# Batch 0 and the end of chunk 0 of a fused attention and GELU-MLP kernel: TensorE's order written anew

## The chip, the cores and the metric

The kernel runs on one core of one Trainium2 chip. The metric is the device time of one execution in microseconds (us). The six runs of the kernel before lie between 326.59 and 328.40 us, with a median of 327.44 us.

## The reference

```python
# q, k, v: (8, 8, 576, 64), s: (8, 8, 576): batch, head, position, width
scores = q @ k^T / 8
cum    = cumsum(max(s, 0))                       # along the positions
scores = where(causal, -1e9, scores + min(cum[j] - cum[i], 0))
attn   = softmax(scores)
x      = (attn @ v) as (4608 tokens, 512)        # token = batch * 576 + position
out    = gelu(x @ w_in) @ w_out                  # w_in: 512 x 2048, w_out: 2048 x 512
```

Eight batches of attention, with a decaying bias, feed a two-layer MLP over 4608 tokens.

## The kernel before, in words

**Attention.** The heads of a batch are taken in four pairs (0 to 3). For a pair, `sc_item` computes the scores, transposed, in two units (u0 and u1), each in a PSUM tile of two banks, tag "sc", of which there are two. ScalarE takes the exponential of each unit (line 415) into a bf16 tile P, and VectorE zeroes what is not causal with a mask (lines 424 and 429). The bias is carried in two weights, `wb` (the exponential of the running sum) and `vv` (v times that). `av_mm` (line 437) then makes either the denominators (P times wb, "den") or the numerators (P times vv, "num"): eight matmuls each for the first 512 positions. `norm_act` takes the denominators on ScalarE through a Ln (two instructions, line 453) and an Exp (line 457), and `norm_dve` (line 480, VectorE, two or three instructions) multiplies numerators by these and writes a pair's rows of `xT`, the input of the MLP. The last 64 positions of a batch are done apart (`av_rest`, `norm_rest`).

With `av_banks(True)`, a pair's numerators and denominators share one "sc" tile (the profile calls it avw). Else they are two one-bank tiles of tag "av" (avn and avd), of which there are three; with `last=True` the numerators take the one bank of tag "mlp". A numerator matmul into an avw tile waits until the Ln has read the denominators out of that tile.

**MLP.** The tokens are cut into nine chunks of 512. `l1_item(c, f2)` (line 541) makes two of the 16 blocks of the hidden layer: 16 matmuls over four rows of `w_in` (row ko needs pair ko of `xT`, and there are two blocks and two column halves e), in an "sc" tile, or with `av=True` in two "av" tiles; a GELU (lines 548, 551) writes them to `gT`. `k0` and `k1` choose rows, so that an item can be made in parts. `l2_item(c, sub, f0, f1)` (line 563) makes 128 rows of the output in a bank, over blocks f0 to f1 of `gT`; `l2_out` copies the bank to SBUF on VectorE (line 573; three buffers o_sb) and stores it through SP's queue (line 575).

**Order.** Nothing is planned by a scheduler: the order in which the program writes instructions is the order of each engine, and each engine runs its own list in order, with semaphore waits where data or a buffer is needed. Attention of batch c+1 is written between the second layer's items of chunk c, so that TensorE has work while ScalarE and VectorE are at the softmax.

- Batch 0 (lines 644 to 653): pairs 0 and 1 use avw tiles, pair 2 avd and avn, pair 3 avd and the "mlp" bank. First the denominators of all, then the numerators of pairs 0, 1, 2, 3, each followed by its `norm_dve`.
- Chunk 0's first layer (lines 657 to 662): two tiles are open, with rows 0 and 1 first, then row 2, then row 3; then the third tile, in the "av" banks.
- Chunk 0's second layer (lines 679 to 743) holds batch 1's attention. Pairs 2 and 3 of batch 1 come at the end (lines 714 to 732).

**The feed of q and k.** From batch 2 on, q and k are loaded (line 105, POOL's queue), interleaved (line 181; batch 2 on POOL, later ones on VectorE), written to DRAM (line 190, SP's queue) and read back transposed into `qkT` (line 197, SP's queue). A tiny POOL copy, `pace`, holds back the next loads: at line 719 until batch 1's last P is masked, at line 740 until the last transposed rows of batch 2 have landed; `load_qk(3)` and `load_v(3)` stand behind that one (lines 741, 742). Batch 3's q is interleaved on VectorE at line 781 in chunk 1, ahead of the masks of the last pair of batch 2.

Of the kernel before, what the change touches and what calls it, by code (L numbers as in the profile page):

```python
# [19 lines left out]
def kernel(  # L20
# [412 lines left out]
    def av_mm(b, p, out, parts, den):  # L433
        for n_part, (jt, lo, n, off) in enumerate(parts):
            for e in range(2):
                h = 2 * p + e
                nc.tensor.matmul(  # L437
                    out[e * 64 : e * 64 + 64, lo : lo + n],
                    lhsT=(
                        wb[:, jt, b * H + h : b * H + h + 1].to_broadcast([128, 64])  # L440
                        if den else vv[b % 2][:, jt, h, :]
                    ),
                    rhs=P_of[b, p][:, e, off : off + n],
                    start=(n_part == 0), stop=n_part == len(parts) - 1,
                    skip_group_check=True,
                )
# [12 lines left out]
    def norm_act(den, w, chunks):  # L459
        ln = norm_ln(den, chunks)  # L460
        norm_exp(ln, w)
        return ln
# [90 lines left out]
    def l2_item(c, sub, f0=0, f1=FT, av=False, defer=False):  # L553

        gT = gT_of[c]
        if f0 == 0:
            tag, bufs = ("av", 3) if av else ("mlp", 1)
            o_of[c, sub] = ps.tile([128, KO * 128], fp32, tag=tag, bufs=bufs, name="o_ps")
        o_ps = o_of[c, sub]
        for ft in range(f0, f1):  # L560
            for e in range(2):
                t0 = sub * 128 + e * 64
                nc.tensor.matmul(  # L563
                    o_ps[e * 64 : e * 64 + 64], lhsT=gT[:, ft, t0 : t0 + 64], rhs=w_out_r[:, ft, :],
                    start=(ft == 0), stop=(ft == FT - 1), skip_group_check=True,
                )
        if f1 == FT and not defer:
            l2_out(c, sub)
# [12 lines left out]
    def gelu_set():  # L581
        nc.scalar.preload_act_table_set("gelu_and_others")
# [63 lines left out]
        av_mm(0, p, avs[p][1], MAIN, True)  # L646
    lns = {p: norm_act(avs[p][1], CUT, CHUNKS) for p in (0, 1)}
    for p in range(NP):
        av_mm(0, p, avs[p][0], MAIN, False)
        norm_dve(0, p, p + 1, avs[p][0], lns[p], 0, CUT, CHUNKS)  # L650
        if p + 2 < NP:
            lns[p + 2] = norm_act(avs[p + 2][1], CUT, CHUNKS)
    gelu_set()

    for c in range(NCH):
        nb = c + 1
        for k0, k1 in ((0, 2), (2, 3)) if c == 0 else ((0, 3),):
            l1_item(c, 0, k0, k1)
            l1_item(c, 1, k0, k1)
        l1_item(c, 0, KO - 1)  # L660
        l1_item(c, 1, KO - 1)
        l1_item(c, 2, av=True)
        if 0 < c and nb < B:
            scale_v(nb, STS, nc.vector)
            absmax_v(nb)
        if c == 0:
            absmax_v(0)
            scale_v(0, STS[ST - 1 :], nc.vector)
        if c < B:
            for p in range(NP):  # L670
                absmax(c, p)
        if 1 < c and nb + 1 < B:
            nc.gpsimd.tensor_copy(pace, qkT[nb % 2][:, 1, NP - 1, 0:1])  # L673
            load_v(nb + 1)
            if nb + 2 < B:
                load_qk(nb + 2)
        for f2 in range(3, FT // 2):
            l1_item(c, f2)
        if c == 0:
            load_v(2)  # L680
            for p in range(NP):
                av_rest(0, p)
            tr_full(1, 0, (nc.vector.tensor_copy, nc.vector.tensor_copy))
            tr_full(1, 1, (nc.scalar.copy, nc.vector.tensor_copy))
            exp_set()
            l2_item(c, 0, 0, 4)
            l2_item(c, 1, 0, 4, av=True)
            norm_rest(0)
            l2_item(c, 0, 4, 8)
            sc_item(1, 0)  # L690
            l2_item(c, 1, 4, 8)
            l2_item(c, 0, 8, 12)
            sc_item(1, 1)
            l2_item(c, 1, 8, 12)
            l2_item(c, 2, 0, 12, av=True)
            scale_pair(1, 0)
            scale_pair(1, 1)
            avs = [av_banks(True) for _ in range(2)]
            for p in (0, 1):
                av_mm(1, p, avs[p][1], MAIN, True)  # L700
            lns = [norm_ln(avs[p][1], CHUNKS) for p in (0, 1)]
            for p in (0, 1):
                norm_exp(lns[p], CUT)
            l2_item(c, 3, 0, 4, av=True)
            for p in (0, 1):
                av_mm(1, p, avs[p][0], MAIN, False)
                norm_dve(1, p, p + 1, avs[p][0], lns[p], 0, CUT, CHUNKS)
            l2_item(c, 3, 4, 8)
            for p in (2, 3):
                tr_full(1, p, (nc.scalar.copy, nc.vector.tensor_copy))  # L710
            scale_pair(1, 2)
            scale_pair(1, 3)
            l2_item(c, 3, 8, 12)
            sc_item(1, 2)
            l2_item(c, 0, 12, defer=True)
            sc_item(1, 3, units=(0,))
            l2_item(c, 1, 12, defer=True)
            sc_item(1, 3, units=(1,))
            nc.gpsimd.tensor_copy(pace, P_of[1, 3][:, 0, UO[1] + 448 : UO[1] + 449])
            interleave(2, "q")  # L720
            interleave(2, "k")
            avs = {}
            for p in (2, 3):
                avs[p] = av_banks(True)
                av_mm(1, p, avs[p][1], MAIN, True)
                ln = norm_act(avs[p][1], CUT, CHUNKS)
                av_mm(1, p, avs[p][0], MAIN, False)
                l2_item(c, p, 12, defer=True)
                l2_out(c, p - 2)
                norm_dve(1, p, p + 1, avs[p][0], ln, 0, CUT, CHUNKS)  # L730
            l2_out(c, 2)
            l2_out(c, 3)
            for i in (0, 1):
                write_rows(2, i, nc.sync)
            for p in (0, 1):
                transpose_rows(2, p)
            gelu_set()
            for p in (2, 3):
                transpose_rows(2, p)
            nc.gpsimd.tensor_copy(pace, qkT[0][:, 1, 3, 0:1])  # L740
            load_qk(3)
            load_v(3)
            absmax_v(1)
        elif nb < B:
            exp_set()
            l2_item(c, 0, 0, 4)
            if c == 1:
                for p in range(NP):
                    av_rest(1, p)
            sc_item(nb, 0)  # L750
            if c == 1:
                norm_rest(1)
            l2_item(c, 0, 4)
            late = c < 3
            for p in range(1, NP):
                if nb + 1 < B and p == 1 and not late:
                    interleave(nb + 1, "q")
                    write_rows(nb + 1, 0, nc.sync)
                if nb + 1 < B and p > 1 and not late:
                    transpose_rows(nb + 1, p - 2)  # L760
                sc_item(nb, p)
                av_item(nb, p - 1)
                if nb + 1 < B and p == NP - 1 and late:
                    interleave(nb + 1, "k")
                    write_rows(nb + 1, 1, nc.sync)
                l2_item(c, p, 0, 12)
                if p == NP - 1:
                    if nb + 1 < B:
                        for pt in range(0 if late else p - 1, NP):
                            transpose_rows(nb + 1, pt)  # L770
                    if c == 1:
                        nc.gpsimd.tensor_copy(pace, qkT[(nb + 1) % 2][:, 1, p, 0:1])
                        load_qk(nb + 2)
                    av_item(nb, p)
                    norm_rest(nb)
                    gelu_set()
                l2_item(c, p, 12)
                if nb == B - 1 and p == 1:
                    cert_decay()
                if nb + 1 < B and p == 2 and late:  # L780
                    interleave(nb + 1, "q")
                    write_rows(nb + 1, 0, nc.sync)
                if nb + 1 < B and p == 1 and not late:
                    interleave(nb + 1, "k")
                    write_rows(nb + 1, 1, nc.sync)
        else:
            if c == B - 1:
                cert_1()
            for sub in range(4):
                if c == NCH - 1 and sub == 2:  # L790
                    break
                l2_item(c, sub, av=sub % 2 == 0)
                if c == B - 1 and sub < 3:
                    (cert_2, cert_3, cert_4)[sub]()
# [174 lines left out]
```

## Time and profile before

| what | value |
|---|---|
| median of 6 runs | 327.44 us (326.59 to 328.40) |
| the profiled execution | 328.12 us, its span 326.1 us |
| granted TensorE clock, mean | 0.999 |
| PE busy | 315.5 us, 97% of the span |
| ACT busy | 204.0 us, 63% |
| DVE busy | 191.9 us, 59% |
| DMA over the span, HBM | 164 GB/s |

PE is TensorE's matmuls, PEld its weight loads, DVE VectorE, ACT ScalarE, POOL GpSimd; SPq and POOLq are the sequencers that issue DMAs. A line of the timeline holds the start in us from the span's start, the duration in us, the engine, the program's line and operation, the tiles (out<-in), the count, and in brackets how long the engine had been idle before it and what ended that. In the view of waits a line holds who waited for whom, the total in us, how many times, and the longest. In the chain of work that ended last, each piece is followed back to what released it.

A matmul's end is modelled, so that one group overlaps the next on the page. In the timeline at single instructions, the starts show more: a group of eight numerators or denominators takes 0.38 us from its first start to the next group's, and 128 first-layer matmuls take 13.81 us in the chain, 0.108 each.

### The profile page before, as it was taken

The page shows a single profiled execution, that of the slowest core. Times are in us where ns is not written, and L with a number is a line of the kernel's source. Part 1 is how long each engine was busy: PE and PEld are TensorE (multiplying, and loading weights), DVE is VectorE, ACT ScalarE, POOL GpSimd, SP SyncE. Part 2 cuts the span into 40 slices and gives each one's busy share as a digit, 9 for nine tenths or more (in the row PEclk, how much of TensorE's full clock was granted, in tenths as well). Part 3 has the DMA queues.
Part 4 walks back from the last instruction along what each step waited for, and adds up shares of the span by engine and source line. Part 5 has one row for each costly group of instructions (what it writes and reads, how often), then busy time and mean ns, then how long its engine had stood idle before and what let it go on. Part 6 is the DMA issues. An engine that isn't in the chain of part 4 may idle for free.

```text
span 326.1 us, 8609 instructions
## 1 busy us (share of the span) xinstructions
PE 315.5 (97%) x3681; PEld 184.4 (57%) x3681; DVE 191.9 (59%) x380; ACT 204.0 (63%) x290; POOL 70.9 (22%) x107
## 2 busy tenths in 40 slices
PE   7999998999999999999999999999999999999994
PEld 3666664666655556556655665556555655455553
DVE  6876558895589247936494749555874672150011
ACT  4896757659576857677667767676759676105400
POOL 8745364304400361008005300410000000000000
PEclk9999999999999999999999999999999999999999
DMA  7999999764985599977995997677600100010012
GB/s 116 213 208 212 232 197 230 276 112 49 255 268 94 110 220 261 216 134 195 252 198 150 206 242 112 121 211 175 111 32 34 66 35 2 32 66 33 3 66 72
DMA packets 53869, 47.45 MB, mean 146 GB/s; under 512 B 31360, under 2 KB 43904, under 8 KB 53824
## 3 DMA queue, kind: packets, MB, share of 16 engines
q0 software_dynamic: 15968, 23.07, 38.4%
q1 hardware_dynamic: 37856, 23.75, 29.8%
q8 instruction: 31, 0.51, 0.7%
q14 instruction: 14, 0.11, 0.1%
HBM read 36.85 MB, written 16.52 MB: 164 GB/s over the span
## 4 chain that ended last, share of the span: by engine, by line
PE 92%; ACT 3%; DMA 2%; POOL 1%; DVE 1%; issue 0%; POOLq 0%
PE h_ps L541 38%; PE o_ps L563 36%; PE sc_ps L399 5%; PE avd L437 3%; PE avn L437 3%; PE lo_ps L809 2%; DMA early_k<-in_q_dram 2%; PE avw L437 1%; PE avr L437 1%; ACT P L415 1%; POOL early_q L117 1%; ACT ln L453 1%; PE tr_ps L363 1%; DVE qkT L384 0%; PE trf_ps L380 0%
## 5 line engine op out<-in xcount | busy, mean ns | idle before, releaser
L563 PE MATMUL o_ps<-w_out_r,gT 128*64 128x512 bf16 x1088 | 126.5, 380 | 0.0
L541 PE MATMUL h_ps<-xT,w_in_r 128*64 128x512 bf16 x1152 | 126.0, 379 | 0.0
L541 PEld LDWEIGHTS <-w_in_r 128*64 128x64 bf16 x1152 | 68.6, 110 | 55.6 <-issue 0.2
L548 ACT ACTIVATE gT<-h_ps 128x1024 bf16<-128x1024 f32 x54 | 54.3, 1023 | 53.8 <-PE h_ps L541 53.8
L563 PEld LDWEIGHTS <-gT 128*64 128x64 bf16 x1088 | 59.4, 110 | 47.5 <-issue 0.2
L415 ACT ACTIVATE P<-sc_ps 128x1024 bf16<-128x1024 f32 x64 | 62.3, 1021 | 26.6 <-PE sc_ps L399 26.1
L424 DVE TENSOR_TENSOR P<-P,tri_bf 128x512 bf16<-128x512 bf16 x59 | 24.6, 423 | 43.7 <-ACT P L415 43.4
L573 DVE COPY o_sb<-o_ps 128x512 f32<-128x512 f32 x34 | 23.4, 687 | 44.4 <-PE o_ps L563 44.2
L216 DVE TENSOR_REDUCE amx<-qkT 128x2 f32<-128x1152 bf16 x32 | 40.9, 1335 | 0.0
L205 POOL DMA_DIRECT2D raw_v<-in_v_dram x40 | 34.3, 882 | 6.9 <-DMA w_in_r<-in_moe_w_in_dram 3.4
L480 DVE SCALAR_TENSOR_TENSOR xT<-avn,ln 128x256 bf16<-128x256 f32 (+3 forms) x60 | 20.2, 383 | 20.1 <-ACT ln L457 14.3
L233 DVE TENSOR_TENSOR vv<-raw_v,wb 128x512 bf16<-128x512 f32 (+3 forms) x44 | 25.3, 633 | 0.1
L223 DVE TENSOR_REDUCE amv<-raw_v 128x1 f32<-128x2048 f32 (+1 forms) x16 | 23.0, 1471 | 3.4 <-DMA raw_v<-in_v_dram 3.4
L457 ACT ACTIVATE ln<-ln 128x512 f32<-128x512 f32 (+1 forms) x40 | 23.4, 588 | 1.2
L551 ACT ACTIVATE gT<-h_ps 128x512 bf16<-128x512 f32 x36 | 19.6, 602 | 6.3 <-PE h_ps L541 6.3
L399 PE MATMUL sc_ps<-qkT 64*128 64x256 bf16 (+2 forms) x320 | 21.3, 250 | 0.7 <-DVE qkT L384 0.3
L399 PEld LDWEIGHTS <-qkT 64*128 64x128 bf16 x320 | 13.0, 94 | 15.2 <-issue 12.8
L453 ACT ACTIVATE ln<-avd 128x256 f32<-128x256 f32 x52 | 17.2, 391 | 6.3 <-PE avd L437 6.3
L437 PEld LDWEIGHTS <-vv 128*64 128x64 bf16 x384 | 17.8, 110 | 3.7 <-issue 2.7
L437 PEld LDWEIGHTS <-wb 128*64 128x64 bf16 x384 | 17.1, 110 | 4.0 <-issue 0.3
L673 POOL CAST pace<-qkT 128x1 f32<-128x1 bf16 x4 | 0.8, 199 | 69.6 <-DMA qkT<-rows 69.6
L437 PE MATMUL avd<-P,wb 128*64 128x256 bf16 x208 | 14.8, 264 | 0.0
(106 smaller groups left out, 184.2 us busy)
## 6 DMA issues: line engine op xcount, KB each, us to landing
out_dram<-o_sb SPq DMA_DIRECT2D x34, 256.0 KB, 2.6
raw_v<-in_v_dram POOLq DMA_DIRECT2D x32, 256.0 KB, 8.4
rows<-qk_bf SPq DMA_DIRECT2D x12, 576.0 KB, 6.7
early_q<-in_q_dram POOLq DMA_DIRECT2D x13, 288.0 KB, 9.5
early_k<-in_k_dram POOLq DMA_DIRECT2D x12, 288.0 KB, 10.0
w_in_r<-in_moe_w_in_dram POOLq DMA_DIRECT2D x4, 512.0 KB, 11.5
w_out_r<-in_moe_w_out_dram POOLq DMA_DIRECT2D x4, 512.0 KB, 12.8
raw_v<-in_v_dram POOLq DMA_DIRECT2D x8, 128.0 KB, 9.4
```

The costliest lines, as they stand in the source:

```text
L205: nc.gpsimd.dma_start(out=t[:n_st, st, :, :], in_=bass.AP(tensor=v.tensor, offset=v.offset + b * H * S * D + st * 128 * D, ap=[[D, n_st], ...
L216: nc.vector.tensor_reduce(amx[:, b * NP + p], qkT[b % 2][:, :, p, :S], axis=AX, op=ALU.max, apply_absolute_value=True)
L233: eng.tensor_tensor(vb[:n_st, st0:st1, h0:h1, :], t[:n_st, st0:st1, h0:h1, :], wb[:n_st, st0:st1, b * H + h0 : b * H + h1] .unsqueeze(3).t ...
L399: nc.tensor.matmul(s_ps[:, e, off : off + n], lhsT=qkT[b % 2][e * 64 : e * 64 + 64, 1, p, jt * 128 : jt * 128 + 128], rhs=qkT[b % 2][e * 6 ...
L415: nc.scalar.activation(P[:, :, UO[u] : UO[u] + UW[u]], s_ps[:, :, : UW[u]], func=AF.Exp, scale=scale)
L424: eng.tensor_tensor(d, d, tri_bf.unsqueeze(1).unsqueeze(1).to_broadcast([128, 2, 2, 128]), op=MULT)
L437: nc.tensor.matmul(out[e * 64 : e * 64 + 64, lo : lo + n], lhsT=(wb[:, jt, b * H + h : b * H + h + 1].to_broadcast([128, 64]) if den else ...
L457: nc.scalar.activation(ln[:, :w], ln[:, :w], func=AF.Exp, scale=-1.0)
L541: nc.tensor.matmul(h_of[c, f2][i][e * 64 : e * 64 + 64], lhsT=w_in_r[:, ko, ft * 128 + e * 64 : ft * 128 + e * 64 + 64], rhs=xT[:, ko, c * ...
L548: nc.scalar.activation(gT_of[c][:, f2 * 2 : f2 * 2 + 2, :], hh_of[c, f2], func=AF.Gelu)
L563: nc.tensor.matmul(o_ps[e * 64 : e * 64 + 64], lhsT=gT[:, ft, t0 : t0 + 64], rhs=w_out_r[:, ft, :], start=(ft == 0), stop=(ft == FT - 1), ...
L573: nc.vector.tensor_copy(o_sb, o_ps)
```

## The change

Three places of the written order change; no instruction is added or removed, and the instructions on VectorE, ScalarE, GpSimd and SP keep their order. Only TensorE's list is in another order.

1. Batch 0: the numerators of pair 2 come ahead of those of pair 1.
2. Chunk 0's first layer: rows 0, 1 and 2 one by one over the two open tiles, and the third tile is opened, with its row 0, ahead of row 3.
3. End of chunk 0: the last four blocks of output sub-block 1 are cut in two, with the scores of pair 3's second unit between them. Both avw tiles of pairs 2 and 3 are taken ahead of the loop; the last quarter of output 2 goes between the two groups of denominators, and that of output 3 between the two groups of numerators.

```diff
     for p in range(NP):
-        av_mm(0, p, avs[p][0], MAIN, False)
+        if p != 2:
+            av_mm(0, p, avs[p][0], MAIN, False)
         norm_dve(0, p, p + 1, avs[p][0], lns[p], 0, CUT, CHUNKS)
         if p + 2 < NP:
             lns[p + 2] = norm_act(avs[p + 2][1], CUT, CHUNKS)
+        if p == 0:
+            av_mm(0, 2, avs[2][0], MAIN, False)
     gelu_set()
...
-        for k0, k1 in ((0, 2), (2, 3)) if c == 0 else ((0, 3),):
+        for k0, k1 in ((0, 1), (1, 2), (2, 3)) if c == 0 else ((0, 3),):
             l1_item(c, 0, k0, k1)
             l1_item(c, 1, k0, k1)
+        if c == 0:
+            l1_item(c, 2, 0, 1, av=True)
         l1_item(c, 0, KO - 1)
         l1_item(c, 1, KO - 1)
-        l1_item(c, 2, av=True)
+        l1_item(c, 2, 1 if c == 0 else 0, av=True)
...
             sc_item(1, 3, units=(0,))
-            l2_item(c, 1, 12, defer=True)
+            l2_item(c, 1, 12, 14)
             sc_item(1, 3, units=(1,))
+            l2_item(c, 1, 14, defer=True)
             nc.gpsimd.tensor_copy(pace, P_of[1, 3][:, 0, UO[1] + 448 : UO[1] + 449])
             interleave(2, "q")
             interleave(2, "k")
-            avs = {}
+            avs = {p: av_banks(True) for p in (2, 3)}
+            lns = {}
             for p in (2, 3):
-                avs[p] = av_banks(True)
                 av_mm(1, p, avs[p][1], MAIN, True)
-                ln = norm_act(avs[p][1], CUT, CHUNKS)
-                av_mm(1, p, avs[p][0], MAIN, False)
-                l2_item(c, p, 12, defer=True)
-                l2_out(c, p - 2)
-                norm_dve(1, p, p + 1, avs[p][0], ln, 0, CUT, CHUNKS)
+                lns[p] = norm_act(avs[p][1], CUT, CHUNKS)
+                if p == 2:
+                    l2_item(c, 2, 12, defer=True)
+            l2_out(c, 0)
+            av_mm(1, 2, avs[2][0], MAIN, False)
+            l2_item(c, 3, 12, defer=True)
+            norm_dve(1, 2, 3, avs[2][0], lns[2], 0, CUT, CHUNKS)
+            l2_out(c, 1)
+            av_mm(1, 3, avs[3][0], MAIN, False)
+            norm_dve(1, 3, 4, avs[3][0], lns[3], 0, CUT, CHUNKS)
             l2_out(c, 2)
             l2_out(c, 3)
```

## The prediction

> **What bounds the kernel now.** I read first the page's busy times and the chain that ended last, to see which engine decides; then the waits and the timeline of the two stretches that the change touches; then the waits after them, to see what a shift of TensorE would run into.
>
> From the page:
>
> ```profile
> PE 315.5 (97%) x3681; PEld 184.4 (57%) x3681; DVE 191.9 (59%) x380; ACT 204.0 (63%) x290; POOL 70.9 (22%) x107
> ...
> PE 92%; ACT 3%; DMA 2%; POOL 1%; DVE 1%; issue 0%; POOLq 0%
> ```
>
> TensorE is 92% of the chain: work taken out of its idle time moves the end, unless something later waits for what did not move. The waits of the whole run, and then of 44 to 62 us:
>
> ```profile
> PE avw L437 <- ACT ln L453: 2.3, 3, 1.2
> ```
> ```profile
> PE avw L437 <- ACT ln L453: 1.9, 2, 1.2
> ```
>
> Numerators waiting for the Ln of their own tile: once in batch 0, twice at the end of chunk 0. The timelines of 9 to 22 us and of 44 to 62 us show where:
>
> ```profile
> 18.25 0.57 PE L437 MATMUL avw<-P,vv 128*64 128x256 bf16 x8 [0.42 <-ACT ln L453]
> 18.25 1.12 PEld L437 LDWEIGHTS <-vv 128*64 128x64 bf16 x23 [0.56 <-issue]
> 18.63 0.96 PE L437 MATMUL avn<-P,vv 128*64 128x256 bf16 x16
> ```
> ```profile
> 55.14 0.57 PE L437 MATMUL avw<-P,vv 128*64 128x256 bf16 x8 [1.16 <-ACT ln L453]
> ...
> 57.71 0.57 PE L437 MATMUL avw<-P,vv 128*64 128x256 bf16 x8 [0.75 <-ACT ln L453]
> ```
>
> By first starts of single matmuls the holes are larger, since modelled ends cover some: 17.61 to 18.25, 53.76 to 55.14 and 56.74 to 57.71. Less the 0.05 that a half-width matmul takes in a full stream: 0.59, 1.33 and 0.91 us. And one row of chunk 1 (timeline 58 to 96 us), which matters below:
>
> ```profile
> 89.16 0.83 DVE L181 COPY qk_bf<-early_q 128x1152 bf16<-128x1152 bf16 x2 [0.61 <-DMA early_q<-in_q_dram]
> ```
>
> **Parts 1 and 2: batch 0 and the first layer.** Pair 2's numerators (0.38 us) need no Ln, and their vv is scaled by 17.44, so they fit into the 0.59 hole; pair 1 still starts at 18.25, when its Ln (ended 18.20) lets it. The first layer could then start at 19.01 instead of 19.39. Two things hold it. The first quarter of w_in landed at 18.99, so it starts at about 19.04. Then, by single rows, the second tile is opened after four matmuls instead of later, and its buffer is pair 1's avw tile, free when `norm_dve` of pair 1 ends at 19.69; the row before shows TensorE let off at 19.74. By 19.74 the old order has issued two first-layer matmuls, the new one four: 2 x 0.108 = 0.22 us ahead. Row 2 comes at 21.03 (pair 2 of xT is ready at 20.86); without the third tile row 3 would come at 21.89 and wait for pair 3, ready at 22.06 (old row 3 starts at 22.11, just behind it), and the 0.22 would be lost again. The third tile's row 0, four matmuls of 0.108, is the cover: row 3 comes at 22.32. That tile's banks are pair 2's, released at 20.86; its w_in quarter landed at 21.58, so 0.3 us of cover. Sum: 0.22; ends 0 (w_in lands late) and 0.38 (no hold).
>
> **Part 3: the end of chunk 0,** in times of the profile before.
> - Old: second unit's scores of pair 3 at 53.08, Exp at 53.52. New: half of output 1's last quarter (0.46 us with the restart) ends at 52.55, scores 52.65 to 52.97; the Exp starts at 53.13, when ScalarE is free: 0.39 earlier. Pair 2's Ln then ends at 54.70 (old 55.09).
> - Second half 52.97 to 53.42; denominators of pair 2 to 53.80; output 2's quarter (8 x 0.108 = 0.86) to 54.66. Denominators of pair 3: their tile is the second unit's, free at 54.2; from the fifth matmul (54.87) they need its mask, which starts when the Exp ends (54.15) and takes 0.42: 54.6. Done by 55.05.
> - Numerators of pair 2 at 55.05 (Ln over at 54.70, so 0.3 of cover); output 3's quarter 55.43 to 56.29; pair 3's Ln starts at 55.29, behind its denominators, and its two instructions end at 55.95: 0.3 of cover. Numerators of pair 3 to 56.67.
> - Chunk 1's first layer starts at 56.67, old 58.95: **2.28 us.** It is late next at its second tile, 12 matmuls on (57.97), which reuses pair 3's tile: `norm_dve` runs 56.93 to 57.69, on a VectorE that has copied outputs 0 and 1 by 57.0. No wait. Bounds: if a cover fails, one hole returns (0.9 or 1.3 us).
>
> The switches between scores and other matmuls, 0.09 to 0.10 each, are as many as before. Nothing is queued anew on VectorE, ScalarE, POOL or SP, whose lists are unchanged.
>
> TensorE enters chunk 1 **0.22 + 2.28 = 2.50 us** earlier.
>
> **What is late next.** The feed of q and k does not gain as much. Follow SP's queue: stores of outputs 0 to 3, then the writes of batch 2's rows at 61.08, then eight transposed reads, each about 1.3 us of issue, the last landing at 77.22; `pace` at 77.34; loads of batch 3. Output 3's copy waits for an o_sb buffer, that is for the landing of output 0's store (59.87; the copy starts at 59.99). That store is issued 0.6 us earlier (0.39 + 0.22), among the same loads of v, and I take its landing, and all behind it, as 0.5 us earlier (ends 0 and 0.9).
>
> Chunk 1's sc_items keep their room: pair 1's transposed rows land at 72.8, needed at 77.5 - 2.5; the others have more. VectorE's list there is full from 60.6 to 74.29 and then waits 2.16 for the first Exp of batch 2; with the list 0.3 earlier and TensorE 2.5 earlier nothing of that is left, but the later mask has 0.49 more.
>
> The loads of batch 3 decide. q's second load landed at 88.97 and VectorE had waited 0.61 us for it (the last row above). Behind that interleave stand, in VectorE's list, the masks of pair 3 of batch 2, then `norm_dve` of pair 2, whose num bank TensorE needs for pair 3's numerators. From the interleave's start: masks at 89.91 (two copies, 0.37 apart), 90.24, 90.58, then norm from 90.71, 0.82 long, ending at 91.53, TensorE let off at 91.58. Old start of those numerators: 92.31, of which 0.12 was a wait behind the Ln and Exp that held the norm to 91.43; that moves with TensorE. So TensorE can move by 92.31 - 91.58 = 0.73 us, and beyond that only as far as the load does.
>
> How far does the load move? By the feed's 0.5, and by what shares its engines. Output 0's store of chunk 1 was issued at 79.14 and landed at 86.35, 7.2 us for 256 KB, inside the loads' landings (84.7 to 90.7), where one alone took 2.0 (59.77 to 61.77). 2.5 us earlier it goes ahead of the loads, whose bytes move from about 81.5 on: 256 KB at the 217 to 291 GB/s of 82 to 89 us is about 1.1 us less. The stores of outputs 1 and 2 (83.57, 88.58) slide into the window and give half back. Estimate 0.5; ends -0.5 and 1.1.
>
> [...]
>
> So TensorE keeps min(2.50, 0.73 + 0.5 + 0.5) = **1.73, say 1.8 us**: about 0.7 goes into a new wait at 89 to 91 us. Later chunks hold the shift: batch 4's q lands at 120.2, needed at 122.6, and the transposed rows of batches 3 to 7 land 3 to 8 us ahead of their scores.
>
> **The sum.** Profiled execution 328.12 - 1.8 = 326.3. That execution lies 0.68 above the median of the six, so on the median: 327.44 - 1.8 = **325.6 us.** A measurement of this kernel tells about 0.3%, 1 us, from no change.
>
> **Rivals.**
> - A, the feed keeps up (0.20): store and loads move together by 1.8 or more, and all 2.50 stays: 324.9. For: the load's landing depends on stores that all come earlier. Against: transposed reads are bound by issue, not by TensorE.
> - B, the feed stands still (0.20): output 0's store lands when it did, since v's loads (last landing 58.77) hold the engines, and the stores give nothing: TensorE keeps 0.73: 326.7, within 0.3%. For: that store took 4.1 us. Against: the Exp and masks before it do move.
> - C, slower (0.05): the stores of chunk 1, all 2.5 us earlier, go ahead of q's loads on the engines and push the second load back. Price: 0.73 minus the delay, one for one, since masks and norm stand behind the interleave. It decides from 0.73; two whole stores (2 x 1.1) make 0.73 - 2.2 = -1.5: 328.9.
> - D, the holes are refilled with waits and little is gained (0.05): pair 3's denominators or the w_in quarter come late, one large hole stays, and the feed eats the rest: 327.0.
> - Forecast (0.50): 325.6.
>
> **Chances.** Faster by over 0.3%: forecast and A, and a little of B, 0.72; within: most of B and D, 0.22; slower: 0.06. The range leaves out C and what lies beyond A and D: from 324.9 down 0.4 for the spread of runs, 324.5, and from 326.7 up 0.5, 327.2.
>
> **What would show it.** No wait of avw for Ln above 0.1 us from 44 to 62 us; chunk 1's first layer at about 56.4 instead of 58.95; batch 0's first layer at about 19.0, third tile's row at about 21.9. VectorE's wait before the q interleave in chunk 1 above 0.61 (about 2 us), and a new idle piece of TensorE before the numerators of pair 3 of batch 2 of about 0.7. Wrong if TensorE idles anew in 53 to 58 us, or if that q load lands later than 88.97.

## The result and the profile after

The median of 32 runs is 325.54 us; that of 69 runs of the kernel before, on the same chips, is 327.67. The ratio is 0.9939 [0.9927, 0.9951]: by it the change takes 2.0 us off, with an interval of 1.6 to 2.4 (the two medians differ by 2.13). The forecast was 325.6, that is 1.8 less. The profiled execution took 326.39 us, its span 324.4, at a clock of 0.998; it lies 0.85 above its median, and the wait for w_out below belongs to that execution.

The page of the changed kernel, busy times and the chain by engine:

```profile
PE 315.5 (97%) x3681; PEld 180.7 (56%) x3681; DVE 191.4 (59%) x380; ACT 203.7 (63%) x290; POOL 71.1 (22%) x107
...
PE 75%; DMA 14%; DVE 5%; POOL 3%; issue 1%; ACT 0%; POOLq 0%; ACTq 0%; DVEq 0%
```

The work is the same, but the chain now runs through DMAs for 14%, before for 2%: followed back from the end it runs into w_out's load and from there into the loads of the first 50 us. The waits of 44 to 62 us name it, and no longer hold a row of avw waiting for an Ln (before: 1.9 us):

```profile
PE o_ps L563 <- DMA w_out_r<-in_moe_w_out_dram: 1.0, 1, 1.0
```

The timeline of 9 to 22 us (start, duration, engine, line, what, count, idle before it):

```profile
17.60 0.58 PE L437 MATMUL avn<-P,vv 128*64 128x256 bf16 x8
18.21 0.57 PE L437 MATMUL avw<-P,vv 128*64 128x256 bf16 x8
...
18.98 3.29 PE L541 MATMUL h_ps<-xT,w_in_r 128*64 128x512 bf16 x26
...
19.70 2.30 PEld L541 LDWEIGHTS <-w_in_r 128*64 128x64 bf16 x24 [0.58 <-DVE xT L480]
```

Pair 2's numerators stand in the hole at 17.60, the first layer starts at 18.98 (forecast about 19.0), and the weight loads stop until 19.70 for pair 1's `norm_dve`: the hold at the second tile that the forecast priced. The timeline of 50 to 60 us:

```profile
51.63 1.05 PE L563 MATMUL o_ps<-w_out_r,gT 128*64 128x512 bf16 x8 [1.00 <-DMA w_out_r<-in_moe_w_out_dram]
...
55.91 0.55 PE L437 MATMUL avw<-P,vv 128*64 128x256 bf16 x8
...
57.15 0.55 PE L437 MATMUL avw<-P,vv 128*64 128x256 bf16 x8
...
57.54 2.76 PE L541 MATMUL h_ps<-xT,w_in_r 128*64 128x512 bf16 x24
```

Both groups of numerators come without a wait, so the two holes of part 3 are gone. But the first matmul on w_out's last quarter stood 1.0 us for its load, which landed at 51.59 (before at 48.74). Nothing in the forecast looked at that load. And from the timeline of 58 to 96 us:

```profile
62.07 0.69 DVE L573 COPY o_sb<-o_ps 128x512 f32<-128x512 f32 x1 [2.89 <-DMA out_dram<-o_sb]
...
76.30 0.75 DVE L424 TENSOR_TENSOR P<-P,tri_bf 128x512 bf16<-128x512 bf16 x2
...
78.16 3.64 PE L563 MATMUL o_ps<-w_out_r,gT 128*64 128x512 bf16 x32 [0.20 <-DVE o_sb L573]
...
88.30 0.83 DVE L181 COPY qk_bf<-early_q 128x1152 bf16<-128x1152 bf16 x2 [0.75 <-DMA early_q<-in_q_dram]
```

VectorE stands 2.89 us for the store of output 0 before it can copy output 3; its list is then late for the first mask of chunk 1 (76.30), and TensorE loses 0.42 us at 76 to 78 us (c2-c1 in the table below: 35.17, before 34.75). The q load that was to decide landed at 88.11, and TensorE, already late, does not wait for it.

### The profile page after: what moved, and what is told of

It is laid out like the page before. It is cut to its first block, busy times and chain, and to the rows that moved or that the text cites. A ratio compares the mean times of both kernels' runs of the same rounds, so it can differ in the third digit from the quotient of the medians.

```text
span 324.4 us, 8608 instructions
## 1 busy us (share of the span) xinstructions
PE 315.5 (97%) x3681; PEld 180.7 (56%) x3681; DVE 191.4 (59%) x380; ACT 203.7 (63%) x290; POOL 71.1 (22%) x107
## 4 chain that ended last, share of the span: by engine, by line
PE 75%; DMA 14%; DVE 5%; POOL 3%; issue 1%; ACT 0%; POOLq 0%; ACTq 0%; DVEq 0%
PE o_ps L563 32%; PE h_ps L541 30%; DMA w_in_r<-in_moe_w_in_dram 4%; PE sc_ps L399 4%; DMA raw_v<-in_v_dram 4%; DMA w_out_r<-in_moe_w_out_dram 4%; PE avd L437 3%; PE avn L437 3%; PE lo_ps L820 2%; DMA out_dram<-o_sb 2%; DVE amv L223 2%; DVE amx L216 1%; POOL raw_v L205 1%; DVE vv L233 1%; PE avr L437 1%; DVE o_sb L573 1%
## 5 line engine op out<-in xcount | busy, mean ns | idle before, releaser
L541 PEld LDWEIGHTS <-w_in_r 128*64 128x64 bf16 x1152 | 65.1, 110 | 59.0 <-DVE xT L480 0.6
```

Of the source, the lines that this page charges most:

```text
L541: nc.tensor.matmul(h_of[c, f2][i][e * 64 : e * 64 + 64], lhsT=w_in_r[:, ko, ft * 128 + e * 64 : ft * 128 + e * 64 + 64], rhs=xT[:, ko, c * ...
```

## The experiments

The same work starts up to 3 us earlier or later from one execution to the next (n0 below lies at 17.01 to 20.00 us). So stages are compared by distances within a trace: n0 is the first start of batch 0's numerators; c0, c1 and c2 are the first matmuls of the first layer of chunks 0, 1 and 2. From c2 to the last matmul it is 227.36 to 227.38 us in every trace: a gain that reaches c2 stays, and the time is settled before it.

| kernel | c0-n0 | c1-n0 | c2-c1 | c2-n0 |
|---|---|---|---|---|
| before | 2.14 | 41.70 | 34.75 | 76.45 |
| after, first profile | 1.76 | 40.32 | 35.17 | 75.49 |
| e1_repeat (after) | 1.76 | 39.23 | 35.10 | 74.33 |
| e11_repeat2 (after) | 1.76 | 39.22 | 34.73 | 73.95 |
| e2_part3_only | 2.14 | 39.44 | 34.98 | 74.42 |
| e3_parts12_only | 1.76 | 41.49 | 34.75 | 76.24 |
| e9_no_third | 1.76 | 39.43 | 34.73 | 74.16 |
| e4_osb4 | 1.76 | 39.22 | 34.73 | 73.95 |
| e5_q_after | 1.76 | 39.22 | 34.73 | 73.95 |
| e6_q_after_osb4 | 1.93 | 39.39 | 34.73 | 74.12 |
| e10_best_again (as e6) | 1.76 | 39.22 | 34.73 | 73.95 |
| e8_before_osb4 | 2.14 | 41.71 | 34.75 | 76.46 |
| e12_wout_late | 1.77 | 44.43 | 34.73 | 79.16 |
| e7_v_first | 2.14 | 39.31 | 40.53 | 79.84 |

My theory after the first profile: the holes are closed for their forecast size, and what is missing was lost in three places behind them, at w_out, at the o_sb buffer and at the q load. For the wait on w_out there were two explanations: **X**, it belongs to that execution, whose loads were late, and **L**, the change brings it, as TensorE reaches the weights earlier.

### The changed kernel again (e1_repeat)

No edit.

> The changed kernel again, for a second profiled execution. In the first one TensorE was 1.2 us ahead at the end of chunk 0 instead of 2.5, since the last quarter of w_out landed at 51.6 (48.7 in the profile before) and output 0's last quarter waited 1.0 us for it. Theory L (the wait belongs to the order: TensorE now comes before the loads): the wait is there again, 0.8 us or more, and chunk 1's first layer starts near 57.5. Theory X (the loads of that one execution were late): no such wait, chunk 1's first layer starts at 56.4 to 56.7, and the loss is in chunk 1, at the q interleave of batch 3. Time by both about 325.5.

Median 325.55, ratio 0.9922 [0.9891, 0.9954]. The waits and the timeline of 44 to 62 us of e1_repeat:

```profile
DVE o_sb L573 <- DMA out_dram<-o_sb: 2.5, 1, 2.5
```
```profile
51.08 1.05 PE L563 MATMUL o_ps<-w_out_r,gT 128*64 128x512 bf16 x8
...
55.35 0.55 PE L437 MATMUL avw<-P,vv 128*64 128x256 bf16 x8
...
56.60 0.55 PE L437 MATMUL avw<-P,vv 128*64 128x256 bf16 x8
...
56.98 5.35 PE L541 MATMUL h_ps<-xT,w_in_r 128*64 128x512 bf16 x48
```

No bracket at 51.08: w_out's quarter had landed at 49.75. So X holds: of three profiles of the changed kernel only the first shows this wait, and none of the seven edits of it below that have part 3 and leave w_out's loads alone shows it. The distances say the same: this row starts 33.33 us after n0, in before 33.53 (50.78), only 0.2 earlier, since part 3 comes behind it; what moved in the first profile is the landing, 2.85 later than in before. c1-n0 is 39.23, that is 2.47 below before's 41.70, where 2.50 was forecast. VectorE's wait for the store of output 0 is there again (2.51). And from the timeline of 76 to 94 us of the same run:

```profile
88.27 0.83 DVE L181 COPY qk_bf<-early_q 128x1152 bf16<-128x1152 bf16 x2 [1.64 <-DMA early_q<-in_q_dram]
...
89.82 0.81 DVE L480 SCALAR_TENSOR_TENSOR xT<-avn,ln 128x256 bf16<-128x256 f32 x3
...
90.69 0.57 PE L437 MATMUL avn<-P,vv 128*64 128x256 bf16 x8 [0.26 <-DVE xT L480]
```

This is the new wait of the forecast, read bottom up: numerators behind a norm, the norm behind masks and the interleave, the interleave behind the q load. VectorE waited 1.64 us (about 2 forecast), TensorE 0.31 more than the 0.12 of before (0.7 forecast).

### Part 3 alone (e2_part3_only)

```diff
-        if p != 2:
-            av_mm(0, p, avs[p][0], MAIN, False)
+        av_mm(0, p, avs[p][0], MAIN, False)
...
-        if p == 0:
-            av_mm(0, 2, avs[2][0], MAIN, False)
...
-        for k0, k1 in ((0, 1), (1, 2), (2, 3)) if c == 0 else ((0, 3),):
+        for k0, k1 in ((0, 2), (2, 3)) if c == 0 else ((0, 3),):
...
-        if c == 0:
-            l1_item(c, 2, 0, 1, av=True)
...
-        l1_item(c, 2, 1 if c == 0 else 0, av=True)
+        l1_item(c, 2, av=True)
```

> The end of chunk 0 in the new order, batch 0 and the first layer in the old one. By the prediction's sum part 3 is 2.28 us of 2.50 ahead of the loads, and what the feed lets through decides: about 0.2 us slower than the changed kernel, ratio to the kernel before about 0.994. Rival: the loads alone decide the end of chunk 0, so that parts 1 and 2 add nothing: the same as the changed kernel, 0.9935 to 0.9945.

Median 325.85, ratio 0.9947 [0.9925, 0.997]. c1-n0 39.44: part 3 is worth 41.70 - 39.44 = 2.26 us in the trace (2.28 forecast), nearly all of the change.

### Parts 1 and 2 alone (e3_parts12_only)

```diff
-            l2_item(c, 1, 12, 14)
+            l2_item(c, 1, 12, defer=True)
             sc_item(1, 3, units=(1,))
-            l2_item(c, 1, 14, defer=True)
...
-            avs = {p: av_banks(True) for p in (2, 3)}
-            lns = {}
+            avs = {}
             for p in (2, 3):
+                avs[p] = av_banks(True)
                 av_mm(1, p, avs[p][1], MAIN, True)
...
```

> Batch 0 and the first layer in the new order, the end of chunk 0 in the old one. By the prediction 0.22 us less, ratio 0.9993, the first layer starting at 19.0 with a hold at its second tile until about 19.7. Rival (the hold at w_in or at pair 1's tile takes all): ratio 1.000.

Median 327.58, ratio 0.9995 [0.9982, 1.0008]. The trace has 41.70 - 41.49 = 0.21 us (0.22 forecast); the interval of the time, 0.4 us to either side, does not tell it from nothing.

### Without the third tile ahead (e9_no_third)

```diff
-        if c == 0:
-            l1_item(c, 2, 0, 1, av=True)
         l1_item(c, 0, KO - 1)
         l1_item(c, 1, KO - 1)
-        l1_item(c, 2, 1 if c == 0 else 0, av=True)
+        l1_item(c, 2, av=True)
```

> The changed kernel without the third tile opened ahead of row 3 of the first layer. By the prediction the 0.22 us of parts 1 and 2 are lost again, in a wait of about 0.22 us ahead of row 3 (pair 3 of xT is ready some 4.8 us after the first numerators start): the distance from the first numerators to chunk 1's first layer is 39.45 instead of 39.23. In the time that is less than the runs can tell. Rival: row 3 needs no cover, the distance stays at 39.23.

Median 325.18, ratio 0.994 [0.992, 0.9961], not to be told from e11_repeat2 on the same chip (0.9946 [0.9928, 0.9964]). In the trace c1-n0 is 39.43 against 39.22: the 0.21 of parts 1 and 2 is lost again, as the forecast said of this case. Timeline of 17 to 24 us of e9_no_third, pair 3's `norm_dve`, which ends at 21.96, and the weight loads of row 3 behind it:

```profile
21.20 0.76 DVE L480 SCALAR_TENSOR_TENSOR xT<-avn,ln 128x256 bf16<-128x256 f32 x2 [0.45 <-ACT ln L457]
...
22.01 2.08 PEld L541 LDWEIGHTS <-w_in_r 128*64 128x64 bf16 x21 [0.29 <-issue]
```

### A fourth o_sb buffer (e4_osb4, and on the kernel before e8_before_osb4)

```diff
-        o_sb = work.tile([128, KO * 128], fp32, tag="osb", bufs=3, name="o_sb")
+        o_sb = work.tile([128, KO * 128], fp32, tag="osb", bufs=4, name="o_sb")
```

> The changed kernel with four o_sb buffers instead of three, so that output 3's copy at the end of chunk 0 waits for no store. In the changed kernel's profile that copy started at 62.07, 2.9 us after VectorE was free, and VectorE's list (74.3 before, 76.4 after) then made the masks of batch 2 late: about 0.4 us on TensorE at 76 to 78 us. Theory V (VectorE's list held by the store): those 0.4 us go, the row writes are issued by 60, and the time falls by 0.4 to 1.0 against the changed kernel, ratio 0.991 to 0.993. Rival: TensorE only runs into the q load of batch 3 instead, and the time stays at 0.994.

> The kernel before with four o_sb buffers. There output 3's copy waited only 0.24 us for a store and VectorE had 2 us to spare at 74 us, so by theory V nothing changes: ratio 0.999 to 1.001. Rival (the buffer is worth something by itself): 0.998 or less.

e4: median 325.13, ratio 0.9921 [0.9897, 0.9946]. e8: 327.67, ratio 1.0000 [0.9981, 1.0018]. Timeline of 54 to 96 us of e4_osb4:

```profile
60.19 1.28 DVE L573 COPY o_sb<-o_ps 128x512 f32<-128x512 f32 x2
...
88.72 0.82 DVE L181 COPY qk_bf<-early_q 128x1152 bf16<-128x1152 bf16 x2
```

The copies of outputs 2 and 3 stand back to back, without the 2.5 to 2.9 us, and c2-c1 is 34.73. But in this execution output 0's store landed at 60.87, about when the second copy began, so three buffers would hardly have waited either; and its clock was halved at 10.92 to 17.75 us, ahead of n0 (mean clock of that run 0.987). The proof is e10 below, also with four buffers (its timeline of 54 to 96 us):

```profile
57.73 1.28 DVE L573 COPY o_sb<-o_ps 128x512 f32<-128x512 f32 x2
```

There the two copies stand back to back until 59.01, and output 3's store is issued at 59.04, while output 0's store lands only at 60.39. So the store's late landing is what held VectorE. In the kernel before, where that wait was 0.2 us, the fourth buffer is worth nothing (e8). The time of e4 lies 0.4 us under that of e1, inside both intervals.

### The q interleave behind the masks (e5_q_after), and with four buffers (e6, e10)

```diff
                 if nb + 1 < B and p == NP - 1 and late:
+                    interleave(nb + 1, "q")
+                    write_rows(nb + 1, 0, nc.sync)
                     interleave(nb + 1, "k")
...
-                if nb + 1 < B and p == 2 and late:
-                    interleave(nb + 1, "q")
-                    write_rows(nb + 1, 0, nc.sync)
```

e6 and e10 are one kernel: this edit with the one of e4.

> The changed kernel with the q interleave of batch 3 (and of batch 4) moved on VectorE's list from ahead of the last pair's masks to behind the norm of pair 2, next to the k interleave. In the repeat's profile TensorE lost 0.31 us at 90.7 because masks and norm stood behind that interleave, which waited 1.64 us for its load. Theory Q (the prediction's new wait): the wait of TensorE ahead of pair 3's numerators falls to the old 0.12 in every execution, VectorE no longer waits over 0.7 us for that load, and up to 0.3 us are won: 325.3. Rival: the interleave is then so late that batch 3's rows or the norm of pair 3 hold TensorE, 0 to 1 us slower than the changed kernel.

> The same, with four o_sb buffers as well. If the two held all that the changed kernel loses in chunk 1, the distance from chunk 1's first layer to chunk 2's is back at 34.7 us (34.75 in the kernel before, 35.1 to 35.2 in the two profiles of the changed kernel), all 2.5 us stay, and the ratio is 0.992 to 0.9925. Rival: something else of the feed comes next and the distance stays at 35.0 or more.

> The changed kernel with the q interleave behind the masks and the norm, and four o_sb buffers, beside the changed kernel on the same chip: 34.73 us from chunk 1's first layer to chunk 2's again, and 0.2 to 0.6 us faster than the changed kernel, ratio to the kernel before 0.991 to 0.9925. Rival: the two are worth nothing in the median, as the changed kernel loses there only in executions with late loads: 0.9935 to 0.9945.

e5: median 325.85, ratio 0.9942 [0.9923, 0.996]. e6: 325.04, 0.991 [0.9884, 0.9936]. e10: 325.2, 0.9944 [0.9924, 0.9963]. Timeline of 76 to 104 us of e5_q_after:

```profile
89.04 0.82 DVE L480 SCALAR_TENSOR_TENSOR xT<-avn,ln 128x256 bf16<-128x256 f32 x3 [0.65 <-ACT ln L457]
89.78 0.82 DVE L181 COPY qk_bf<-early_q 128x1152 bf16<-128x1152 bf16 x2
...
89.92 0.57 PE L437 MATMUL avn<-P,vv 128*64 128x256 bf16 x8
```

The norm comes ahead of the interleave, as the edit says, and the numerators follow with no bracket: c2-c1 is 34.73 in e5, e6 and e10. But none of the three tests the wait. The q load landed 68.9 to 69.9 us after n0 there, in e1 70.3; e9, without the edit and with its load at 68.95, has 34.73 as well. (e6 gave up 0.17 in batch 0: pair 1's numerators waited for their Ln until 1.16 us after n0, in the first profile until 0.99. Its w_in quarter had landed at 19.04, ahead of the first layer at 19.26.) The time does not show a gain either: e10 has 0.9944, and e11, the unedited kernel on the same chip, 0.9946; in e11's own trace nothing is lost at these places either (34.73). Whether e6 beats the changed kernel by 0.2 us or not at all stays open.

### The changed kernel a third time (e11_repeat2)

> The changed kernel once more, for the comparison and a third profile. 39.2 us from the first numerators to chunk 1's first layer if the last quarter of w_out lands by 50.7, more by what it is later; 34.75 to 35.2 from there to chunk 2's; ratio 0.9935 to 0.994.

Median 325.44, ratio 0.9946 [0.9928, 0.9964]; all 2.50 us reach c2 (76.45 - 73.95). There the q load landed at 87.87, 68.70 after n0, in before's profile 71.72.

### q and k behind v (e7_v_first): the price of a late load

```diff
-            load_qk(3)
             load_v(3)
+            load_qk(3)
```

> The changed kernel with the v loads of batch 3 issued ahead of its q and k loads at the end of chunk 0: q's second load then lands some 4 us later (1.15 MB of v at about 288 GB/s). By the prediction's rule TensorE keeps 0.73 us plus the load's shift against the old 89.0: with the load at about 92 that is -2 to -3, so TensorE waits 3 to 5 us ahead of pair 3's numerators and the kernel is slower than the kernel before by 0.6 to 1%. Rival (masks and norm are not what counts): no such wait, time as the changed kernel.

Median 333.18 of four runs (330.66 to 336.40); the ratio, without the longest, is 1.0193 [1.0144, 1.0242], more loss than the 0.6 to 1% expected. The profiled execution is the shortest of the four. The timeline of 84 to 98 us:

```profile
92.01 0.83 DVE L181 COPY qk_bf<-early_q 128x1152 bf16<-128x1152 bf16 x2 [6.11 <-DMA early_q<-in_q_dram]
...
93.32 0.96 PE L437 MATMUL avd<-P,wb 128*64 128x256 bf16 x8 [4.00 <-DVE P L424]
...
94.43 0.96 PE L437 MATMUL avn<-P,vv 128*64 128x256 bf16 x8 [0.15 <-DVE xT L480]
...
95.41 1.60 PE L563 MATMUL o_ps<-w_out_r,gT 128*64 128x512 bf16 x8
```

The load landed at 91.93, 2.96 later than before's 88.97. The forecast's chain from interleave to numerators then lets TensorE off at 91.58 + 2.96 = 94.54; it was 94.43. So the order of that chain is right (TensorE's long wait stands one step earlier than expected, ahead of pair 3's denominators, for a mask of the same chain). What the expectation missed is the duration 1.60 in the last row, for eight matmuls that take 1.03 to 1.05 elsewhere. The windows of the same trace, with the granted clock in the third column from the end:

```profile
88.00:89.30 1.30, 1.30 (x14) 0.45 (x8) 0.00 (x0) 0.71 (x2) 0.00 (x0) 1.00 1.23 213
89.30:93.30 4.00, 0.02 (x2) 0.01 (x1) 1.29 (x4) 0.00 (x0) 0.00 (x0) 0.98 0.73 155
93.30:95.40 2.10, 1.93 (x24) 1.49 (x26) 1.81 (x7) 1.05 (x3) 0.00 (x0) 0.50 0.74 281
95.40:97.00 1.60, 1.60 (x18) 0.74 (x16) 1.24 (x4) 1.55 (x4) 0.00 (x0) 0.63 0.61 223
97.00:99.00 2.00, 2.00 (x22) 0.99 (x18) 1.94 (x4) 0.78 (x1) 0.00 (x0) 1.00 0.76 190
```

After 4 us of idle the clock is halved: the means of the second and fourth row (0.98 and 0.63) put its fall at about 93.15 and its return at 96.6, 3.4 us. Matmuls ran in it from 93.32 on, for 3.3 us at half speed: 1.6 lost. With the idle time by starts, 4.17, that is 5.8; c2-c1 grew by 40.53 - 34.73 = 5.80.

### w_out's last quarter behind two more loads (e12_wout_late)

```diff
+    for n in "qk":
+        load_early(2, n, 0)
     load_w(1, 3)
-    load_qk(2)
+    for n in "qk":
+        load_early(2, n, 2)
```

> The changed kernel with the last quarter of w_out loaded behind the first two loads of batch 2's q and k, so that it lands some 2.9 us later (about 51.5 to 52.6). By the reading of the first profile, output 0's last quarter, which TensorE reaches at 50.3 to 51.1, then waits for it in every execution, 1 to 2 us, and that is lost from the 2.5: ratio 0.996 to 1.000. Rival (that wait in the first profile had another cause): no wait, 0.994.

Median 328.48, ratio 1.0032 [1.0007, 1.0058], slower than the kernel before; 0.996 to 1.000 was expected. Timeline of 47 to 58 us and windows of the profiled execution (330.19 us, above its median):

```profile
53.01 1.92 PE L563 MATMUL o_ps<-w_out_r,gT 128*64 128x512 bf16 x8 [2.29 <-DMA w_out_r<-in_moe_w_out_dram]
...
56.93 1.07 PE L563 MATMUL o_ps<-w_out_r,gT 128*64 128x512 bf16 x4
```
```profile
51.50:52.00 0.50, 0.00 (x0) 0.00 (x0) 0.50 (x3) 0.50 (x1) 0.00 (x0) 1.00 1.14 151
52.00:52.50 0.50, 0.00 (x0) 0.00 (x0) 0.50 (x3) 0.04 (x1) 0.00 (x0) 0.90 1.30 190
52.50:53.00 0.50, 0.00 (x0) 0.00 (x0) 0.17 (x2) 0.00 (x0) 0.00 (x0) 0.50 1.25 215
...
58.50:59.00 0.50, 0.50 (x8) 0.26 (x6) 0.50 (x3) 0.17 (x1) 0.18 (x2) 0.50 0.58 107
59.00:59.50 0.50, 0.50 (x6) 0.25 (x4) 0.26 (x1) 0.50 (x2) 0.50 (x2) 0.77 0.22 57
59.50:60.00 0.50, 0.50 (x10) 0.37 (x8) 0.00 (x0) 0.47 (x2) 0.50 (x1) 1.00 0.11 33
```

The quarter landed at 52.97. TensorE stood 2.45 us by starts, less than in e7, yet the clock stays halved for longer: the means of 0.90 and 0.77 put its fall at 52.4 and its return at 59.2. c1-n0 is 5.2 above that of e1: 2.45 of idle and up to (59.2 - 53.0) / 2 = 3.1 of half speed. The mean clock of the whole run tells how often this happens: 0.99 in 2 of the 10 runs, 0.993 to 0.995 in 6, and 1.0 in the two fastest (326.0 and 326.9 us). In 145 runs of the other kernels beside it (all but e7) it is 0.983 to 0.990 in seven and never 0.991 to 0.995. The changed kernel's wait that ends at 51.63 is of the same kind, but shorter: there the idle time was 1.2 by starts, and the clock stayed at 1.00.

## Why the prediction was right

**Parts 1 and 2, 0.22.** Right: 0.21 in e3, by the hold at the second tile until 19.70. Two of its conditions held as well: without the third tile the gain is lost (e9), and where w_in lands late it shrinks (in e7 the first layer waited for it until 19.15, c0-n0 2.14, and c1-n0 is 0.09 longer).

**Part 3, 2.28.** Right: 2.26 in e2. No cover failed: in 44 to 62 us of after and e1 no numerators wait for an Ln.

**"VectorE's list ... the later mask has 0.49 more."** This step failed. It took the list as 0.3 earlier; the copy of output 3 waited 2.5 to 2.9 us for output 0's store, the list was later instead, and TensorE lost 0.07 (e1) to 0.42 us (after). The loss goes with that wait: none where it is 1.58 (e5) or 1.61 us (e9), 0.07 at 2.51 (e1), 0.25 at 2.70 (e2), 0.42 at 2.89 (after). e10 shows that a fourth buffer takes the wait away.

**The feed's 0.5 earlier, and the stores' 0.5.** Neither gain is shown. Relative to n0, in us earlier than in before's one profile (minus is later):

| term | forecast | e1 | after | e11 | e8 | e3 |
|---|---|---|---|---|---|---|
| batch 2's last transposed row | 0.5 | -0.75 | -1.91 | 1.73 | 0.53 | 0.95 |
| q load, from that row to its landing | 0.5 | 2.14 | 2.74 | 1.29 | 1.80 | 1.94 |
| q load, sum | 1.0 | 1.39 | 0.83 | 3.02 | 2.33 | 2.89 |

e8 and e3 keep TensorE's old order at the end of chunk 0, and their load lands 2.3 and 2.9 us earlier all the same. So the spread between executions is larger than either term, and the profile that the forecast was read from had the latest landing of the 12 traces in which no edit holds the loads back (71.72 us after n0, the others 67.0 to 70.9).

For the first term, the landings are those of rival B: output 0's store lands when v's loads end. Why it does, no trace shows. In 14 traces it took 2.1 to 5.8 us from issue, but always landed 0.67 to 1.43 us after the last v load of batch 2. In e1 it was issued 0.60 us earlier than before, as forecast, and landed 0.68 later: the earlier issue bought nothing. For the second, the store of output 0 of chunk 1 does run ahead of q's loads now (78.14 to 81.55 in after, 3.4 us; before 79.14 to 86.35, 7.2 us). But batch 3's second q load took 6.8 to 8.3 us from issue in the three profiles of the changed kernel, and 7.6 and 7.8 in e3 and e8, where that store still took 6.4 to 7.0 us among the loads; the 9.6 of before is the exception. So the runs do not tell the 1.1 of the forecast for one store from nothing.

**The rule "0.73 plus the load's shift".** Right where the load decides: in e1, 0.73 + 1.39 = 2.12 allowed, and c2 came 76.45 - 74.33 = 2.12 earlier; in e7 off by 0.11. But the 0.73 and the 88.97 are those of one execution. In e8 the same load landed 69.39 after n0, not 71.72: that would be 0.73 + 2.33 = 3.1 us of room, more than the 2.50, and in e3 3.6. In e4, e9 and e11 the load cost nothing. So the forecast's main loss is real but not in every execution, and the median kept 2.0 instead of 1.8. That 1.8 came so near is in part luck: the same rule read from e8's profile, with no shift at all, would have given the whole 2.50. Rival A's 2.50 happened in single executions (e11), not at the median (interval 1.6 to 2.4); B's landing was right and its price wrong; C and D did not occur.

**w_out.** The forecast did not ask when this load lands. In before it landed at 48.74 and was needed at 50.78: 2.0 us of room, of which the change takes 0.2. The first profile of the changed kernel used up all of it by a later landing and lost 1.1 us. That is a loss of one execution, not of the change: it stands in one of the ten traces that have part 3 and w_out's loads as they were.

What stays open: how much of the 2.50 the median loses at each of the three places, or whether it loses 0.5 there at all, since one profile per kernel can't give their frequency (e10, whose trace loses nothing, has a ratio of 0.9944 too); and why a load of one execution lands up to 3 us after the same load of another.

## What to carry to other kernels

A hole that TensorE spends waiting for its own tile's Ln can be filled from the written order, and its worth can be read to 0.03 us from first starts of single instructions. What the gain runs into next is read worse from one profile: list every load, store and buffer that the moved engine reaches earlier, with its room, and compare the room with how much that landing varies between executions, here 1 to 3 us. A late load is not always priced by its idle time alone: behind 2.45 and 4.17 us of idle the traces show matmuls at half speed, behind 1.2 to 1.4 us they do not, and no trace lies between.

## What the runs showed of the hardware

**The clock after an idle stretch.** Idle of 1.2 to 1.4 us by starts left the clock at 1.00 (before at 53.8, after at 50.4). After idle of 2.45 us it was halved for 6.8 us (e12), after 4.17 us for 3.4 us (e7): the shorter idle stretch had the longer halving. In e7 the mean clocks of the runs go with their times: 0.995 at 330.7 us, 0.99 at 332.4 and 334.0, 0.985 at 336.4. A long idle stretch is not the only thing that halves it: in e4 the clock was halved from 10.92 to 17.75 us, 6.83 us, though from 5 to 11 us no two starts of matmuls lie more than 0.82 us apart; the other traces kept 1.00 in that stage.

Nor does the busy share just ahead of a fall sort the cases: the 3.4 us ahead of it were 43% busy in e12 and 82% in e4, while the 3.4 us from 54.0 in before, 53% busy, kept 1.00. In e12 the clock fell 1.87 us after the start of the last matmul (50.53 to 52.4) and stayed halved until 59.2, though TensorE was idle only for the first 0.6 us of that. What decides when the clock falls and for how long stays open: no run shows it.

**Stores behind a backlog.** The time of a 256 KB store from issue to landing ranged from 2.1 to 5.8 us in 14 traces for the same store of the same chunk, and it always landed 0.67 to 1.43 us after the last v load of batch 2.
